# Grouped attention scores, with the main product on half of TensorE's rows, and a new order table

## The chip, the core and the metric

The kernel runs on one core of a Trainium2 chip. The metric is the device time of one launch in microseconds (us). TensorE (PE) does the matmuls, VectorE (DVE), ScalarE (ACT) and GpSimd (POOL) the elementwise work, and SyncE (SP) issues the DMA transfers. Each engine takes its own instructions in program order.

## What is computed

Pooled attention (query rows averaged in pairs) for 4 batches of 8 heads, 1152 keys, 576 pooled queries and head size 64. A feed-forward layer with a squared ReLU follows on 2304 tokens, 512 -> 2048 -> 512.

```python
q_pool = q.reshape(B, H, S // 2, 2, D).mean(axis=3)
scores = scale * np.matmul(q_pool, k.transpose(0, 1, 3, 2))
scores = scores - np.max(scores, axis=-1, keepdims=True)
attn = np.exp(scores)
attn = attn / (np.sum(attn, axis=-1, keepdims=True) + 1e-09)
x = np.matmul(attn, v)          # then heads side by side: (2304, 512)
h = x @ w_in
g = np.maximum(h, 0.0) ** 2
out = g @ w_out
```

## The kernel before, in words

The heads are handled in 16 pairs (pair n is two heads of one batch), and each pair in 9 chunks of 128 query rows, 144 chunks in all. Four chunks belong to the first head and four to the second; the ninth (`CH[j] is None`, here called the mixed chunk) holds the last 64 rows of each head. To keep float32 accuracy on float16 matmuls, numbers are split into a high and a low half (`hi`, `lo`). For keys, `k2` holds both halves beside each other, and a transposing DMA (KT) makes `kT`, in which each block of 128 keys has the 64 `hi` components on partitions 0 to 63 and the 64 `lo` components on 64 to 127. `qT` exists twice (index l): l = 0 as hi over lo, l = 1 with the halves swapped (made by the copies QX). So a full 128-row matmul with l = 0 gives hi x hi + lo x lo, and one with l = 1 gives lo x hi + hi x lo.

For one chunk the steps are: S (`scores`, L656 to L679, scores into one of two PSUM tiles `s0`, `s1` of three banks each), MX (L685, DVE, row maximum), MB (a small bias), EX (L709, ACT, exponential into P and row sums), HI and LO (L713 and L721, split of P), TR (L724, transposing DMA into PT). After four or five chunks a group PV (L869) multiplies PT by V; its two heads write to the two column halves of the array in turn. Pair 0 uses float32 scores (`scores4`, L653) in which two chunks, one of each head, lie on the two row halves of the array; pairs 1 to 15 use `scores`. In pairs 0 to 3 the transposition of P is done by TensorE (L750) and not by DMA. In `scores` a plain chunk has six matmuls of 512, 512, 128, 512, 512 and 128 columns. A mixed chunk has twelve, each with 64 stationary columns, and the two heads alternate matmul by matmul.

Since S alternates between `s0` and `s1`, S of chunk i waits for EX of chunk i - 2 (`back`).

The feed-forward work comes in 9 blocks of 256 tokens: normalisation (RV, RT L926, RB L948, XR L960, XQ L972, XN L980, XA, XD), eight H steps (L1033, 24 matmuls each) and eight O steps (L1082, 12 matmuls each). A block can start when all pairs that it needs are done, so it fills TensorE's time beside later chunks. XN needs XQ, XQ needs both XR, and those need both RB.

The order of all steps on all engines is a hand-over table, `ORDER`, three characters for each step (step, engine, buffer). `Plan.order` (L114) reads it; a step's `engs` says which engines it may run on, with planned durations that the kernel itself does not use.

Of the kernel before, what the change touches and what calls it, by code (L numbers as in the profile page):

```python
# [22 lines left out]
def cfg(k, d):  # L23
# [16 lines left out]
    "BU0O-8B7G1mWBF0BVGBH1BG8B80Bd0BIGBWEB9GBO1BeGBA0BP8BB8BQ1BJ0BR8Bm0BK8PrH1nOBfABnGPs0BX01oOPt8BY83S13TG"  # L40
    "Bg0BoDBv01pG3YSBh8BZ1BS0BwGBa8BT8Bb13cFBi0C201qGBj8Bc8Bx9Bk0C3G1r1Bl8CB01sGC48Bp01tJBr1CCGBq8Bs81u0CK0"
    "1vGCDEBy13dGB-01w8CT0BzG3KWB_GBt1CLGO_03eW1x83ZGCUGBu81yOCMACVB3P1P0GC503QG3aGC01Cc0C18C683V13UOC701z8"
    "Cl0C8G3kX3WGPu0PvGC911-83fWCAGPw0PxGCE13gWCFGCG0PyD3bW1_OCI1CHGCmGCJ8Pz03o9P11P-GCn8P_GQ0GQ1GCdGQ3E3XO"
    "208Q4GQ2GCN0CeDP2G3hOD10COG218CP13iGCR0Cu0CQG3jGCW1CS822OCvGCX83lWCf0Ch1Cg8Ci8CY0D2GCo1CZ8CwCCa0CbGD3G"
    "Cp8D80QvGD4A3nGQw0Cj1Qx8D9GD5R3qFCq0DF0Cr8Ck8D6ODAG3r0Cx1DBD3sGCyGCz03_8Cs1DM040G3xOCt8C-8DGGC_141WQ50"
    "D083mWDC8DHG3yGDIA3zGP312383-WDJKDKG248DDG47X42GQ68DNG25OQ78DT0DEW3p8DOGP4GQA0DPADUGQ88D7WDQD3u13tODa0"
    "Q9O3vGQBGQF14483wODVGDRG43ODW9DbGDSWQC8Q-0Dh0QG8Q_GDcOQD8DXOQH8Qy1DiGQK0DLWQI8QEODdAQzG45GR0FDo046GQL8"
    "DjGR11DeBQJG48WQP0R2GDYG4BDQM8DpGDZWDkCP51DfGQQ8Dq8QR8R3G4AGDgWQN8DlHQS8QU0DrADmGDs8QOGDnWQTGE00DtOP6G"
    "QV84DFDv0E1GQW84E1QZ04FGDuWR4GDwG4K84OOR6OE2G4PGQe1Dx8Qa84LGDyC49W4MGE3BDzQE704NWQb8EE0D-OE8GQj0EFGE98"
    "EA9D_WE4MEGOQc8EL0QXGEH8Qk0QYOEMG4WXEBCE5GEIDES04QWQf8ECGEN8Qg8P71EOAEJGE6WQh8EPRETGQiOEUGEQGEV9EZ0EKW"  # L50
    "QdOQl0P88EaG4C8ERWEW84SO4RGEg0EXO4H1EbGQm0EhGEcAEDWR5G4IGEi8EjEEdL4GOEn04a9EeOEu0EoGEYW4T8Qp1QnNEpG4JG"
    "4UGEqB4VGEfWEkAE_0EvGR78P90ElOF0GErC4XWR8GEw8Ex8Qq0F18EsGPA8QoWF2EEyDEtWFD0Qr04ZOFEGF3J4cFEmWEzGF4OF60"
    "FFG4d0Qs0F7GE-W4eGF8G4fG4nOF98R904jO4oGFGCF5WFHE4kGFR0RAGFIOFK0QtIRB8FSG4pWRJ04lG4YWFTGFLGFUDRE1FAC4mW"
    "FM8FBGRC8Ff0RDORF8FVBPB1FCWRG8FWGFN8RHOFgGRK8QuWRL84qO4rGFh8FY0FiD4vXRO0RIG4b8RMGFZGFj9RNOFJWFt0PCGFkO"
    "Fa8FbC4g14hGFm0FcAFXWFOLRT1RP8FnGFPORQ84s8FuGRR8Rd0Fo8FQWRSGFvOFpE4tGRU84uGRV8RY1FlWFdGFw8RWGFxJRXOG50"
    "RZ8FyG4wWFqCF-04iORe8PD14zDG6GFeWFrORf8Ra8F_GRb8Ri0Rg8PEG4yOG08RcGFzWG18RhO4_FRjG501GC051GG7OFsWRn0G89"
    "5AO52O5BGG2EGDGRk8G3OGJ04xWGE8Ro0GFAGKG56OG9BG4WGLGGG8GAGGQ0GMCPF1GRG5CWRl8GS8RmGGN957GGBWGOOGX0PG8Rp0"
    "4-85DGGHOGPWGYGGTE531GUCRq054G5EOGZGGIWRzHGaB58G5F8Gl055GRrNR-0Ge0GmG5IXRt05GGGfG59WGgGRu0GVGGhA5HGGn8"
    "R_8Gb95JWGs0Gi8GcGRv05MERsWGjOGtGGoDGWWRw0GpR5LGGuOGkW5OAGqO5P1Gz05QGPH15RGG-GGvC5VOGdWRxNGwDG_GGxGPI8"
    "GrWH08S20H40S3G5WGH1CS01S1G5Z8H2OT1GGyWS49H5GS515aGH68T20H78HB0S6G5bWS7G5XGH89HI0HCG5KWH9OPJ1S8GS9GHDG"  # L60
    "HJGHEBH3WHFLHK8SB85dG5cGHLASCGHP05YWT38HMOPK8HW0HQG5N8SD0HGOHXGHAWHRGHSCT41HNOSEGHY8T60HZBHd0T7GHHWT5G"
    "SF85S0SAOHk05TGT8ESGOHeG5e8T91SHOSI0HOWHlGHf8HgAHTPTAGTBG5UG5fGHr0SJ85hXHhMSK8SS1HsGHm8HaD5gGSL8Hn8HiG"
    "5iWSN0HbGRyWSMGHy0SO8HUGHcWSP8SX0SQ8HoI5kO5lBHtGHzGST8HjWHpGHuCPL1SRGSU8HvOSV8SYG5nFSWGHVWSZ8HwO5o0I30"
# [12 lines left out]
    "LG8UM8PZ06uWLHA74GL49LNG75GK_WUN8L5G7AOLI8LS0PaGLOCVC1VE0UOOLDW6x8VDGLZ0VFGLJO701LTGVGFUQ071GLU87FXLVE"
# [1294 lines left out]
```

## Time and profile before

| | us |
|---|---|
| median of 3 runs (775.4 to 783.15) | 780.74 |
| the profiled execution | 780.22 |
| its span | 778.1 |
| TensorE busy in the span | 736.7 |
| VectorE busy | 575.2 |
| ScalarE busy | 525.3 |
| GpSimd busy | 329.8 |

The profile is of one execution, whose own time is 2.1 us over its span. A view by stretches gives the busy time of each engine in each; the chain of work that ended last shows what the end depends on; a timeline lists the work of one engine in order of time, neighbours of one line merged, with the idle time ahead of each in brackets and what ended it. "PEclk" is the granted TensorE clock as a share of 2.4 GHz. In a timeline a matmul group's length includes the tail of its last matmul, about 0.16 us, which the next group overlaps; in the chain it does not.

### The profile page before, as it was taken

The numbers are of one execution on the slowest core, as the hardware profiler recorded it, in microseconds if no ns is written. First come the engines' busy times: TensorE is split into PE (matmuls) and PEld (weight loads), VectorE is DVE, ScalarE is ACT, GpSimd is POOL, SyncE is SP. The second block draws the span as 40 slices with busy tenths as digits, with TensorE's granted clock in tenths as the row PEclk, the third lists the DMA queues.
The fourth block names the chain that finished last, engine by engine and source line by source line (L and its number), as shares of the span: only waits on it lengthen the run. The fifth ranks groups of instructions, "written<-read, shape, count | busy, mean of one in ns | idle before, by whom it ended". The sixth has DMA issues, their size and how long they took to land. (4 is left out here: it accounts for less than half of the span.)

```text
span 778.1 us, 15243 instructions
## 1 busy us (share of the span) xinstructions
PE 736.7 (95%) x5998; PEld 485.7 (62%) x5998; DVE 575.2 (74%) x985; ACT 525.3 (68%) x821; POOL 329.8 (42%) x228
## 2 busy tenths in 40 slices
PE   6888899999899999899999999899999999999997
PEld 4555556557655775458666765586567658576763
DVE  4888999889788888789689888899788962404120
ACT  4988978989786887678877885779767732312140
POOL 1533412455365555464632644543476411204141
PEclk9999999999999999989999999999999999999999
DMA  8894782519999999999999999999999927000011
GB/s 282 279 244 136 219 227 89 122 44 194 208 207 206 198 208 201 213 206 183 214 221 214 199 210 192 203 211 208 225 190 188 195 47 131 1 1 14 15 42 40
DMA packets 324840, 128.96 MB, mean 166 GB/s; under 512 B 307104, under 2 KB 307872, under 8 KB 324768
## 3 DMA queue, kind: packets, MB, share of 16 engines
q1 hardware_dynamic: 324768, 127.98, 80.0%
q8 instruction: 47, 0.77, 0.4%
q14 instruction: 25, 0.20, 0.1%
HBM read 45.09 MB, written 4.72 MB: 64 GB/s over the span
## 5 line engine op out<-in xcount | busy, mean ns | idle before, releaser
L709 ACT ACTIVATE buf<-s,ca 128x1152 f32<-128x1152 f32 x144 | 175.2, 1217 | 57.1 <-DVE ca L695 18.6
L685 DVE TENSOR_SCALAR_CACHE_REDUCE s<-s,esc 128x1152 f32<-128x1152 f32 x135 | 190.5, 1421 | 29.1 <-PE s L674 25.7
L1033 PEld LDWEIGHTS <-w 128*128 128x128 f16 x1728 | 167.6, 98 | 26.7 <-issue 2.2
L721 POOL TENSOR_TENSOR buf<-buf,buf 128x1152 f16<-128x1152 f32 x49 | 121.8, 2489 | 100.8 <-ACT buf L713 78.6
L1082 PE MATMUL ba<-w,region 128*128 128x512 f16 x624 | 142.7, 379 | 0.0
L1082 PEld LDWEIGHTS <-region 128*128 128x128 f16 x864 | 82.4, 98 | 93.5 <-issue 1.7
L674 PE MATMUL s<-kT,qT 128*128 128x512 f16 x720 | 136.0, 329 | 1.8 <-ACT buf L709 1.7
L1033 PE MATMUL ba<-region,w 128*128 128x256 f16 x1128 | 129.4, 273 | 0.8 <-ACT region L1043 0.7
L674 PEld LDWEIGHTS <-qT 128*128 128x128 f16 x720 | 63.9, 100 | 58.8 <-issue 8.4
L869 PE MATMUL ba<-PT,v 128*64 128x320 f16 (+1 forms) x1296 | 85.0, 287 | 5.1 <-DMA PT<-buf 5.0
L721 DVE TENSOR_TENSOR buf<-buf,buf 128x1152 f16<-128x1152 f32 x59 | 81.2, 1385 | 9.7 <-ACT buf L713 9.1
L869 PEld LDWEIGHTS <-v 128*64 128x64 f16 x1296 | 70.7, 110 | 19.1 <-issue 9.2
L1060 POOL TENSOR_TENSOR region<-region 128x512 f16<-128x512 f32 x37 | 48.4, 1313 | 69.8 <-DVE region L1056 36.9
L713 ACT ACTIVATE buf<-buf 128x1152 f16<-128x1152 f32 x65 | 74.5, 1155 | 4.7 <-DVE buf L721 1.8
L1048 ACT ACTIVATE region<-region 128x512 f16<-128x512 f32 x72 | 44.2, 623 | 44.0 <-DVE region L1045 43.4
L750 PE MATMUL ba<-ident,buf 128*128 128x128 f32 x324 | 53.5, 289 | 12.6 <-ACT PT L760 5.7
L1082 PE MATMUL bt<-w,region 128*128 128x512 f16 x240 | 53.6, 379 | 0.0
L750 PEld LDWEIGHTS ba<-ident,buf 128*128 128x128 f32 x324 | 34.6, 143 | 29.2 <-ACT PT L760 12.2
L1056 POOL TENSOR_TENSOR region<-region 128x512 f32<-128x512 f32 x21 | 25.1, 1199 | 59.3 <-ACT region L1048 46.1
L1033 PE MATMUL bt<-region,w 128*128 128x256 f16 x408 | 46.0, 273 | 0.0
L760 ACT ACTIVATE PT<-ba 128x384 f32<-128x384 f32 x85 | 39.1, 489 | 9.9 <-PE ba L750 9.0
L282 POOL TENSOR_SCALAR buf<-buf,cols 128x1152 f16<-128x1152 f32 x19 | 26.6, 1400 | 36.8 <-ACT buf L709 19.4
(181 smaller groups left out, 915.6 us busy)
## 6 DMA issues: line engine op xcount, KB each, us to landing
raw<-in_q_dram SPq DMA_DIRECT2D x32, 288.0 KB, 3.8
raw<-in_k_dram SPq DMA_DIRECT2D x15, 576.0 KB, 4.7
region<-in_moe_w_in_dram SPq DMA_DIRECT2D x8, 1024.0 KB, 7.4
w<-in_moe_w_out_dram SPq DMA_DIRECT2D x8, 1024.0 KB, 6.0
raw<-in_v_dram SPq DMA_DIRECT2D x12, 576.0 KB, 4.6
out_dram<-buf SPq DMA_DIRECT2D x22, 128.0 KB, 2.4
v<-in_v_dram SPq DMA_DIRECT2D x4, 576.0 KB, 6.6
out_dram<-half SPq DMA_DIRECT2D x14, 128.0 KB, 2.5
```

What stands on the lines that cost most here:

```text
L674: nc.tensor.matmul(s[:, x, :w], lhsT=qt[:, l].rearrange("p c m -> p (c m)")[:, 128 * c0 + h : 128 * c0 + h + 255 : 2], rhs=rhs, **st)
L685: nc.vector.tensor_scalar(st3(), st3(), sc, 3e38, op0=ALU.mult, op1=ALU.min, accum_out=a[:, x : x + 1])
L709: nc.scalar.activation(P(), st3(), AF.Exp, bias=a[:, 1:2], scale=s1, accum_out=col)
L713: nc.scalar.activation(hl()[:, 0], P(), AF.Copy)
L721: e.tensor_tensor(out=hl()[:, 1], in0=P(), in1=hl()[:, 0], op=ALU.subtract)
L750: nc.tensor.matmul(t[:, y], lhsT=P()[:, c * 128 : (c + 1) * 128], rhs=ident, is_transpose=True, start=(y == 0), stop=(y == 2), skip_group_ ...
L760: nc.scalar.activation(out, t, AF.Copy)
L869: nc.tensor.matmul(px[h * 64 : (h + 1) * 64, 64 * r * (1 - h) : 64 * r * (1 - h) + N], lhsT=vv[:, h, kc, vl, :], rhs=p2(vi, r, h, 9 * pl + ...
L1033: nc.tensor.matmul(ph[:, f2], lhsT=w16[0][:, SLOT[f // 4], wl, a, f % 4 * 128 : (f % 4 + 1) * 128], rhs=xhl()[:, xl, a], start=(i == 0), s ...
L1048: nc.scalar.activation(gt[u][:, 0], rt[u % 2], AF.Square)
L1060: e.tensor_tensor(out=gt[u][:, 1], in0=rt[u % 2], in1=gt[u][:, 0], op=ALU.subtract)
L1082: nc.tensor.matmul(p[:, :DM], lhsT=g[:, gl, f % 2, tt * 128 : (tt + 1) * 128], rhs=w16[1][:, SLOT[f // 4], wl, f % 4], start=(f == 0 and g ...
```

## The change

Six edits. (1) For pairs 4 to 15 (`flip_`) the key blocks are laid out so that even blocks have hi over lo and odd blocks lo over hi (`kz`, used by `ka` and `kd`; the score columns and PV's V blocks are permuted to match, `PERM`). (2) In those pairs two chunks, one of each head, are scored together (`flipped`): first six full 128-row matmuls for the cross terms of both chunks (L730), then six 64-row matmuls for hi x hi, on the row half where that block's hi lies (L739); lo x lo is left out for these chunks. The order of chunks is `ORDF`, the mixed chunk seventh. S of such a group waits for EX of both chunks of the group before. (3) The mixed chunk still has twelve 64-column matmuls, all four products, but in loops with the head outside the column blocks (L722). (4) QX may run on any of three engines in all pairs. (5) Loads from pair 4 on and stores may be issued from ScalarE's queue (`AQ`). (6) A new `ORDER`.

```diff
 ORDER = (
-    "26W27W28W29X2C000W2E12DG2BG2G02F82I12H82K02MW2JG2L881006W02801O03882G2P18AG13W8382QG8408B904G86187G098"
+    "26W27W28W29X00W06W2C02E12DG2BO2G02FG2I12H82MW2K013W2J82L82NX03O01881002804G09882G05O8AG8382P107O0EW840"
...
-    ENG = ("PE", "ACT", "DVE", "POOL", "SP")
+    ENG = ("PE", "ACT", "DVE", "POOL", "SP", "AQ")
...
+    def queue(o):
+        return nc.scalar if o["eng"] == "AQ" else nc.sync
...
+        def kz():
+            return buf("k2", n).rearrange("p (a z d) -> p a z d", a=9, z=4), raw("k", n).rearrange("p (a z d) -> p a z d", a=9, z=2)
+
         def ka(o):
+            if n in flip_:
+                t, r = kz()
+                scaled(o, t[:, :, 0:4:3], r, tl["psc", n][:, 1, 0:1])
+                return
             scaled(o, k2()[:, :, :, 0, :], rk(), tl["psc", n][:, 1, 0:1])
...
-                add(("QX", n, z), {"SP": 850} if n in cfg("QXD", ()) else alt("QX", DVE=470, POOL=1500), [("QT", n)] + old, lambda o, z=z: qx(o, z), need)
+                add(("QX", n, z), {"DVE": 470, "POOL": 1290, "SP": 850}, [("QT", n)] + old, lambda o, z=z: qx(o, z), need)
...
+        def flipped(o):
...
+            full, half = slice(0, 128), (slice(0, 64), slice(64, 128))
+            if CH[j] is None:
+                for l in range(2):
+                    for h in range(2):
+                        for x, par, y, w in ((0, 0, 0, 4), (1, 1, 0, 4), (2, h, 1, 1)):
+                            nc.tensor.matmul(
+                                to(i, x, w)[half[h]], lhsT=qt[:, l, 8, h : h + 127 : 2], rhs=part(n, h, par, y),
+                                start=(l == 0), stop=(l == 1), skip_group_check=True,
+                            )
+                return
+            two = [(y, *CH[chunks[y][1]]) for y in both(i)]
+            for y, h, c0 in two:
+                for x, par, z, w in ((0, 0, 0, 4), (2, h, 1, 1), (1, 1, 0, 4))[:: 1 - 2 * h]:
+                    nc.tensor.matmul(
+                        to(y, x, w), lhsT=qcol(1 - par, full, h, c0), rhs=part(n, h, par, z),
+                        start=True, stop=False, skip_group_check=True,
+                    )
+            (a, ha, ca), (b_, hb, cb) = two
+            for y, h, c0, x, par, z, w in (
+                (a, ha, ca, 0, 0, 0, 4), (a, ha, ca, 1, 1, 0, 4), (a, ha, ca, 2, ha, 1, 1),
+                (b_, hb, cb, 1 - ha, 1 - ha, 0, 4), (b_, hb, cb, ha, ha, 0, 4), (b_, hb, cb, 2, hb, 1, 1),
+            ):
+                nc.tensor.matmul(
+                    to(y, x, w), lhsT=qcol(par, half[par], h, c0), rhs=part(n, h, par, z)[half[par]],
+                    start=False, stop=True, skip_group_check=True,
+                )
...
+        elif n in flip_:
+            if both(i)[0] == i:
+                back = [("EX", y - 2) for y in both(i)]
+                add(("S", i), {"PE": 1665 if len(both(i)) == 2 else 1115}, [("KT", n), ("QX", n, 0), ("QX", n, 1)] + back, flipped, i)
...
+    ORDF = [0, 7, 1, 8, 2, 5, 4, 3, 6]
...
+    flip_ = set(cfg("FLIP", range(4, 16)))
```

On TensorE, the scores of a plain chunk of pair 4 stood before as follows (`s0` and `s1` are the two score tiles; LDWEIGHTS loads the stationary operand of the matmul under it; the last number is the matmul's columns):

```order
L674 LDWEIGHTS qT0_105
L674 MATMUL s0_112<-kT0_103,qT0_105 128x512
L674 LDWEIGHTS qT0_105
L674 MATMUL s0_112<-kT0_103,qT0_105 128x512
L674 LDWEIGHTS qT0_105
L674 MATMUL s0_112<-kT0_103,qT0_105 128x128
```

and the second half of a group of two chunks of the same pair stands now:

```order
L730 MATMUL s1_113<-kT0_103,qT0_105 128x512
L739 LDWEIGHTS qT0_105
L739 MATMUL s0_112<-kT0_103,qT0_105 128x512
L739 LDWEIGHTS qT0_105
L739 MATMUL s0_112<-kT0_103,qT0_105 128x512
L739 LDWEIGHTS qT0_105
L739 MATMUL s0_112<-kT0_103,qT0_105 128x128
L739 LDWEIGHTS qT0_105
L739 MATMUL s1_113<-kT0_103,qT0_105 128x512
L739 LDWEIGHTS qT0_105
L739 MATMUL s1_113<-kT0_103,qT0_105 128x512
```

Both score tiles are now written in one go, and six matmuls of half the rows (L739; by the diff on the upper, lower, upper, lower, upper and lower rows in turn) stand where six full ones stood.

The mixed chunk of pair 4 on TensorE before (by the code, first and second of each equal two are the first and the second head, on the two column halves):

```order
L669 MATMUL s0_112<-kT0_103,qT0_105 64x512
L669 LDWEIGHTS qT0_105
L669 MATMUL s0_112<-kT0_103,qT0_105 64x512
L669 LDWEIGHTS qT0_105
L669 MATMUL s0_112<-kT0_103,qT0_105 64x512
L669 LDWEIGHTS qT0_105
L669 MATMUL s0_112<-kT0_103,qT0_105 64x512
L669 LDWEIGHTS qT0_105
L669 MATMUL s0_112<-kT0_103,qT0_105 64x128
L669 LDWEIGHTS qT0_105
L669 MATMUL s0_112<-kT0_103,qT0_105 64x128
```

and now:

```order
L722 MATMUL s0_112<-kT0_103,qT0_105 64x512
L722 LDWEIGHTS qT0_105
L722 MATMUL s0_112<-kT0_103,qT0_105 64x512
L722 LDWEIGHTS qT0_105
L722 MATMUL s0_112<-kT0_103,qT0_105 64x128
L722 LDWEIGHTS qT0_105
L722 MATMUL s0_112<-kT0_103,qT0_105 64x512
L722 LDWEIGHTS qT0_105
L722 MATMUL s0_112<-kT0_103,qT0_105 64x512
L722 LDWEIGHTS qT0_105
L722 MATMUL s0_112<-kT0_103,qT0_105 64x128
```

The 512, 512, 128 of the first head now stand together, and those of the second head behind them.

At one normalisation in the middle of the program, TensorE's order before had XN (L980) right behind the second RB (L948):

```order
L948 LDWEIGHTS pick_83
L948 MATMUL ba1_115<-ru_3205,pick_83 64x128
L980 LDWEIGHTS ones_80
L980 MATMUL ba1_115<-buf1_94,ones_80 128x256
L980 LDWEIGHTS ones_80
L980 MATMUL ba1_115<-buf1_94,ones_80 128x256
L980 LDWEIGHTS ones_80
L980 MATMUL ba1_115<-buf1_94,ones_80 128x256
L980 LDWEIGHTS ones_80
L980 MATMUL ba1_115<-buf1_94,ones_80 128x256
L926 LDWEIGHTS r2_3365
L926 MATMUL ba0_114<-negid_82,r2_3365 32x128
```

and now, with RB's rows (L1016) ahead of them, a score group and an RT (L994) stand between RB and XN (L1048):

```order
L739 LDWEIGHTS qT0_105
L739 MATMUL s1_113<-kT0_103,qT0_105 128x128
L994 LDWEIGHTS r2_3379
L994 MATMUL ba0_114<-negid_82,r2_3379 32x128
L1048 LDWEIGHTS ones_80
L1048 MATMUL ba1_115<-buf3_96,ones_80 128x256
```

XN has moved behind the scores of two chunks, and RT from behind XN to ahead of it.

## Rows read from the trace of the kernel before

**Rows 1.** The page: the span, and TensorE's busy time, share and matmuls.
```profile
span 778.1 us, 15243 instructions
PE 736.7 (95%) x5998; PEld 485.7 (62%) x5998; DVE 575.2 (74%) x985; ACT 525.3 (68%) x821; POOL 329.8 (42%) x228
```
**Rows 2.** Busy time by stretches of 40 us; its first line names the columns.
```profile
core 0: us, PE busy (x) PEld busy (x) DVE busy (x) ACT busy (x) POOL busy (x), PEclk, DMA share, GB/s
320.00:360.00 40.00, 34.83 (x326) 24.02 (x324) 34.30 (x64) 28.41 (x47) 18.73 (x14) 0.91 1.05 198
```
**Rows 3.** The chain that ended last: start us, length us, engine, tile, line, instructions.
```profile
543.18 0.97 PE s L669 x12
544.15 1.08 PE s L674 x6
...
583.96 1.10 PE s L669 x12
585.05 2.73 PE ba L1033 x24
587.78 0.97 PE s L674 x6
588.75 2.62 PE ba L1033 x24
```
**Rows 4.** TensorE's timeline, first 60 us: start, length, line, shapes, instructions.
```profile
27.53 2.10 PE L653 MATMUL s<-kT,qT 128*128 128x512 f32 x6
...
43.08 2.21 PE L653 MATMUL s<-kT,qT 64*128 64x512 f32 x12
```
**Rows 5.** What TensorE waited for from 200 us on: us, times, longest.
```profile
PE ba L980 <- ACT buf L972: 4.5, 1, 4.5
PE ba L869 <- DMA PT<-buf: 2.4, 2, 2.1
...
PE s L674 <- ACT buf L709: 0.5, 2, 0.3
```
**Rows 6.** TensorE's timeline from 318 to 362 us.
```profile
331.56 1.01 PE L980 MATMUL ba<-buf,ones 128*128 128x256 bf16 x4 [4.52 <-ACT buf L972]
...
332.73 4.02 PE L674 MATMUL s<-kT,qT 128*128 128x512 f16 x12
...
340.68 2.12 PE L674 MATMUL s<-kT,qT 128*128 128x512 f16 x12
...
349.23 0.61 PE L980 MATMUL ba<-buf,ones 128*128 128x256 bf16 x4
```
**Rows 7.** TensorE's timeline from 485 to 545 us.
```profile
498.31 3.85 PE L869 MATMUL ba<-PT,v 128*64 128x320 f16 x53 [2.12 <-DMA PT<-buf]
...
539.32 3.86 PE L869 MATMUL ba<-PT,v 128*64 128x320 f16 x54
```
**Rows 8.** ACT's timeline from 318 to 336 us.
```profile
327.39 1.22 ACT L709 ACTIVATE buf<-s,ca 128x1152 f32<-128x1152 f32 x1 [1.60 <-DVE region L960]
328.51 0.19 ACT L709 ACTIVATION_READ_ACCUMULATOR buf<-s,ca 128x1 f32 x1
...
331.42 0.28 ACT L692 ACTIVATE ca<-ca,cols 128x1 f32<-128x1 f32 x1
```
**Rows 9.** DVE's timeline from 318 to 336 us.
```profile
329.37 1.42 DVE L685 TENSOR_SCALAR_CACHE_REDUCE s<-s,esc 128x1152 f32<-128x1152 f32 x1
330.70 0.14 DVE L685 DVE_READ_ACCUMULATOR s<-s,esc 128x1 f32 x1
```
**Rows 10.** SyncE's timeline from 180 to 660 us.
```profile
180.50 15.05 SPq L724 DMA_TRANSPOSE PT<-buf  x4
...
591.20 30.88 SPq L724 DMA_TRANSPOSE PT<-buf  x10
626.59 1.86 SPq L1106 DMA_DIRECT2D out_dram<-buf  x2
638.66 14.48 SPq L724 DMA_TRANSPOSE PT<-buf  x5
```

More of the change, by code (lines that the diff above doesn't have):

```diff
@@ L357, in prep, with aq @@
         oldv = oldvs[0]
+        def aq(cost):
+            return {"AQ": cost} if n >= NP else {}
         def rk():
@@ L366, in rq, with load_kv @@
             return raw("q", n).rearrange("p (c r d) -> p c r d", c=9, r=2)
-        def load_kv(t, src):
-            nc.sync.dma_start(
+        def load_kv(o, t, src):
+            queue(o).dma_start(
                 out=t.rearrange("p h c d -> p h (c d)"),
@@ L376, in load_q @@
             for h in range(2):
-                nc.sync.dma_start(out=raw("q", n)[h : h + 127 : 2], in_=sv[h])
+                queue(o).dma_start(out=raw("q", n)[h : h + 127 : 2], in_=sv[h])
         prev = [] if not n else [("LQ", n - 1)] if n - 1 in full_v else [("LV", n - 1)]
@@ L678, in scores, with part, qcol, to @@
                             )
+        def part(n, h, par, y):
+            a = [x for x in range(9 * h, 9 * h + 9) if x % 2 == par]
+            a = a[4 * y : 4 * y + 4]
+            return kT(n)[:, a[0] : a[-1] + 1 : 2] if a else None
+        def flipped(o):
+            kt, qt = kT(n), qT(n)
+            def qcol(l, rows, h, c0):
+                return qt[rows, l].rearrange("p c m -> p (c m)")[:, 128 * c0 + h : 128 * c0 + h + 255 : 2]
+            def to(y, x, w):
+                t = sts[y % 2][:, x, : 128 * w]
+                return t.rearrange("p (a b) -> p a b", a=w)
+            full, half = slice(0, 128), (slice(0, 64), slice(64, 128))
[7 more added lines that the diff above has]
+                            )
+                return
+            two = [(y, *CH[chunks[y][1]]) for y in both(i)]
[14 more added lines that the diff above has]
+                )
         def smax(o):
@@ L1105, in st @@
                     ob = out[b_ * T : (b_ + 1) * T].rearrange("(p c) e -> c p e", c=9)
[L1106 removed]
+                    queue(o).dma_start(out=ob[c], in_=t[z * 64 : (z + 1) * 64])
             add(("OD", j, tt), {"DVE": 720}, [("O", j, tt, 3), ("XO", j)], od, at + 12 + 4 * tt, take=(("o", j, tt), ("buf", "half"), cfg("RO", 1)), give=("O", j, tt, 0))
[L1109 removed]
+            add(("ST", j, tt), {"SP": 1300, "AQ": 1400}, [("OD", j, tt)], st, at + 12 + 4 * tt, give=("o", j, tt))
     ring2 = {}
@@ L1281 @@
     lastr = {}
-    for n, pair, js in first + [(p, p, ORD) for p in range(NP, B * NP)]:
+    for n, pair, js in first + [(p, p, ORDF if p in flip_ else ORD) for p in range(NP, B * NP)]:
         p = preps[n]
```

157 lines of the change are left out of this document (81 added, 76 removed).

## Prediction

> **What bounds the kernel now.** I read the busy times first, then the chain that ended last, then TensorE's waits. TensorE is busy for 736.7 us of a span of 778.1 [rows 1], and in the chain its matmuls follow one another without a gap [rows 3]. From 200 us on it waits for little: 4.5 us once for ACT, 2.4 for transposing DMAs, 0.5 for exponentials of earlier chunks [rows 5]. The idle rest of the 41.4 us lies before 200 us and behind the last matmul. So the reader should see a kernel whose length, behind its first quarter, is the sum of its matmuls, and a change is worth what it does to that sum, unless it opens a wait. SyncE is nearly as full: it issues transposes without a pause from 180 us on, and its first long rest stands between 628.5 and 638.7 us [rows 10]. That is slack of 10 us near the end, so SyncE does not set the end yet.
>
> **The scores of plain chunks.** Six matmuls of a chunk take 0.97 us [rows 3]. Pairs 4 to 15 have 12 x 8 = 96 plain chunks: 93.1 us go. In their place come 48 groups. Their six full matmuls have the columns of one chunk: 0.97 x 48 = 46.6 us. Their six half-row matmuls have those columns again, and what they cost depends on whether the two row halves work side by side. The nearest row is the float32 scores of pair 0: one mixed chunk on all rows takes 2.10 us, and two chunks with the same number of columns each, one on either row half, take 2.21 together [rows 4]. Halves do run side by side there. In the new order upper and lower rows alternate, and each half gets 512 + 128 + 512 columns, half of the total; so I take 0.97 / 2 = 0.485 us, 23.3 us in all. The bounds are this and 0.97 us (nothing side by side, 46.6 in all).
>
> **Changes of mode.** A group of six takes 1.08 us when matmuls on column halves stand ahead of it and 0.97 otherwise, and an H step 2.73 and not 2.62 [rows 3]: each change of how the array is divided costs 0.11 us. Along TensorE's order the division (whole, column halves, row halves, small tiles) changes 126 times before and 211 times now, since each new group enters row halves and leaves them again. 85 x 0.11 = 9.4 us. The Trainium skill, TensorEngine Tiling (Array Packing), section Key Properties, speaks against such a change: changing the tiling mode, not just the tile, drains the engine. It gives no price; the trace agrees that there is one, and by its 0.11 us the sum stays as it stands here.
>
> **The mixed chunk.** Before, the heads alternate, two column halves work side by side, and 2304 columns of path take 0.97 us, or 1.10 with a change of mode ahead [rows 3]. Now three matmuls of one head stand together. Does TensorE start a matmul ahead of one that waits? At 331.56 us XN had waited 4.52 us for ACT, and the scores behind it began only at 332.73 [rows 6], although the exponential that they needed had ended at 328.70 [rows 8]. So starts keep to the program's order. Then the first head's 512 and 512 must have been taken before its 128 and the second head's first 512 can run beside each other; only the ends overlap. The path by columns is 1024 + 1024 + 1024 + 1024 + 128 = 4224 and not 2304, which at the same speed is 1.78 us, 0.81 more; twelve chunks: 9.7 us. The bounds are 0 (they overlap as before) and twice 0.97, 11.6 us. I take 9.7, since a queue that holds scores back for 4 us behind a waiting XN will not look ahead here either. The Trainium skill, TensorE: Matmul & The Clock Gate, section on packing small matmuls, says the same: matmuls start and end strictly first in, first out, and only weight loads are pulled ahead. The 4.52 us wait agrees.
>
> Sum on TensorE: 93.1 - 46.6 - 23.3 - 9.4 - 9.7 = 4.1 us less.
>
> **A wait that goes.** The one wait of 4.52 us has a price behind it: the granted clock of that stretch is 0.91 [rows 2], and the next two chunks took 4.02 us where two such chunks take 2.12, and XN 1.01 against 0.61 [rows 6]; that is 2.3 us at the lower of the two levels (1.2 GHz). In the new order a score group (0.97 + 0.485 + 0.22 = 1.7 us) and RT stand between RB and XN, as the last pair of listings shows. If XQ on ACT is as late as before, 2.8 us of wait remain. A wait of 2.12 us elsewhere did not lower the clock: 53 matmuls behind it took 3.85 us, and 54 take 3.86 without one [rows 7]. So I count 1.7 + 2.3 = 4.0 us won; the bounds are 0 (another wait of that length) and 6.8.
>
> **A wait that comes.** A group writes both score tiles, so it needs EX of both chunks ahead. From the end of a group: MX 1.42 + 0.14 us on DVE, twice, then the bias 0.28 and EX 1.22 + 0.19 on ACT [rows 8, 9], 4.8 us; beside a mixed chunk, where one chunk decides, 3.3. I laid the matmuls that stand between successive score groups of pairs 4 to 15 at the durations of their rows against this. Nine of 59 places have too little, together 2.7 us; in some ten more the margin is under 0.6 us, and DVE or ACT will often be in another instruction. Behind the waiting group stand H, O and PV, so TensorE loses all of it. I take 4 us, bounds 0 and 15 (a quarter of a microsecond at every place).
>
> **What costs nothing.** No transfer stands on ScalarE's queue in the new order, so edit 5 does nothing. The copies QX on SyncE grow by five, and transposes that follow a copy become two fewer of some thirty; this is covered by the 10 us rest at the end of SyncE's work [rows 10], and without it would be about 3 us late at the last PV. The key split keeps its element counts. The first four pairs are computed as before in another order; DVE's work there is the same, so I count 0, though ACT has slightly less.
>
> **Sum.** The profiled execution took 780.22 us, 2.1 over its span and 0.5 under the median of 780.74. 780.2 - 4.1 - 4.0 + 4.0 = 776.1 us, against the median 776.6. I predict 776 us.
>
> **Rivals.**
> (a) *The row halves do not run side by side with float16.* For it: no row shows it at float16, where columns pass twice as fast (0.97 us [rows 3] for what takes 2.10 in float32 [rows 4]). Against it: those rows themselves. It costs up to 23.3 us, 776 + 23 = 799; from a fifth of that (4.7 us) on the kernel is no faster than before. This is the slower case. 8%.
> (b) *The mixed chunk overlaps after all.* 9.7 us come back: 766. Against it is the held-back score group. 12%.
> (c) *Score groups wait throughout.* For it: both tiles are taken at once, and SyncE stays full, so a late transpose delays a buffer, then EX, then the next group. The place is each L730; at 0.25 us each, 15 us instead of 4: 787. Against it: ACT is busy for 68% and DVE for 74% [rows 1]. 20%.
> (d) *My sum, with waits between 1 and 8 us:* 773 to 780. 60%.
>
> **How the numbers follow.** A measurement here can tell about 1% from no change, 773 and 788.5 being the marks. Faster is (b), and about a quarter of (d), where the first 200 us gain from ACT's lighter load: 0.12 + 0.16 = 0.28. Slower is (a) and a quarter of (c): 0.13. Within 1%: 0.59. The range leaves out (a) and the outer ends of (b) and (c): 765 to 788; that of the likeliest case alone is 773 to 780.
>
> **What the new profile should show.** L730's and L739's twelve matmuls together 1.56 us in the chain, 1.67 with a change ahead; L739's starts in pairs. L722 at 1.8 to 1.9 us, not 1.1. TensorE's busy time near 733 us. XN's wait under 3 us and a granted clock of 1.00 there. TensorE's waits at L730 for EX (L773 of the new kernel) of 3 to 6 us. What would make me wrong: L739 near 1 us a group, L722 near 1.1, or waits at L730 above 10 us.

## The result

The changed kernel takes 787.67 us (median of 4 runs, 785.8 to 791.4) against 780.73 before (4 runs, 775.4 to 783.15): a ratio of 1.0112, 95% interval 1.0076 to 1.0147. It is slower by about 1%, where 776 us and no change were forecast. The profiled execution is the slowest of the four, 791.4 us with a span of 789.6, against 780.2 and 778.1; the traces are 11.5 us apart where the medians are 7 apart, so the rows below tell places better than sizes.

The page of the changed kernel, the span and TensorE's busy time:

```profile
span 789.6 us, 15253 instructions
PE 729.5 (92%) x5998; PEld 475.2 (60%) x5998; DVE 583.9 (74%) x988; ACT 521.5 (66%) x819; POOL 325.2 (41%) x222
```

TensorE works 7.2 us less than in [rows 1], and its idle time grew from 41.4 to 60.1 us. The busy time by stretches (the first line names the columns), of the changed kernel:

```profile
core 0: us, PE busy (x) PEld busy (x) DVE busy (x) ACT busy (x) POOL busy (x), PEclk, DMA share, GB/s
0.00:200.00 200.00, 170.53 (x1350) 109.60 (x1351) 167.51 (x291) 159.45 (x239) 78.84 (x56) 0.97 0.64 175
200.00:640.00 440.00, 414.60 (x3600) 270.86 (x3598) 368.09 (x613) 326.71 (x525) 218.73 (x139) 0.98 1.07 202
640.00:820.00 180.00, 144.34 (x1053) 94.75 (x1050) 48.26 (x86) 35.32 (x56) 27.61 (x28) 0.99 0.15 32
```

and of the kernel before:

```profile
0.00:200.00 200.00, 173.34 (x1386) 114.42 (x1388) 169.33 (x287) 165.37 (x253) 75.89 (x54) 0.99 0.67 184
200.00:640.00 440.00, 429.84 (x3634) 281.64 (x3631) 369.87 (x637) 330.60 (x521) 223.21 (x145) 0.99 1.06 197
```

In the 440 us in which chunks of pairs 4 to 15 run, TensorE was idle for 10.2 us before and is for 25.4 now. This is where the saving went. What it waits for there (us in all, times, longest), in the changed kernel:

```profile
PE ba L937 <- DMA PT<-buf: 5.7, 6, 2.1
PE s L730 <- ACT buf L773: 4.3, 5, 1.6
PE ba L510 <- DVE region L1113: 3.8, 2, 2.4
PE ba L510 <- DVE ru L1001: 3.1, 1, 3.1
PE ba L937 <- DVE ru L1001: 2.7, 1, 2.7
```

Against [rows 5] the wait of XN (4.5 us) is gone, but P x V (L937) waits more for transposed P, the score groups (L730) for exponentials, and several matmuls for DVE. The new steps themselves are as cheap as hoped. In the chain that ended last, the full and the half-row matmuls of a group (start, length):

```profile
639.24 1.08 PE s L730 x6
640.32 0.60 PE s L739 x6
```

and on TensorE's timeline a mixed chunk:

```profile
353.62 1.18 PE L722 MATMUL s<-kT,qT 128*64 128x512 f16 x12
```

The half rows run side by side: 0.60 us is 0.49 and the 0.11 of a change of mode. The mixed chunk takes 1.11 us from its first matmul to the next step's start at 354.73, no more than before [rows 3]; the 0.8 us that the prediction charged for it do not exist.

### The profile page after: what moved, and what is told of

Its sections match the earlier page's. It is cut to its first block, busy times and chain, and to the rows that moved or that the text cites. A ratio compares the mean times of both kernels' runs of the same rounds, so it can differ in the third digit from the quotient of the medians.

```text
span 789.6 us, 15253 instructions
## 1 busy us (share of the span) xinstructions
PE 729.5 (92%) x5998; PEld 475.2 (60%) x5998; DVE 583.9 (74%) x988; ACT 521.5 (66%) x819; POOL 325.2 (41%) x222
## 5 line engine op out<-in xcount | busy, mean ns | idle before, releaser
L785 POOL TENSOR_TENSOR buf<-buf,buf 128x1152 f16<-128x1152 f32 x63 | 153.9, 2449 | 151.5 <-ACT buf L777 87.9
L773 ACT ACTIVATE buf<-s,ca 128x1152 f32<-128x1152 f32 x144 | 175.3, 1218 | 40.9 <-POOL ca L759 10.8
L1150 PE MATMUL ba<-w,region 128*128 128x512 f16 x576 | 131.1, 379 | 0.7 <-DVE psc L520 0.7
L937 PE MATMUL ba<-PT,v 128*64 128x320 f16 (+1 forms) x1296 | 89.2, 296 | 9.5 <-DMA PT<-buf 5.7
L937 PEld LDWEIGHTS <-v 128*64 128x64 f16 x1296 | 76.2, 114 | 23.5 <-issue 13.5
L777 ACT ACTIVATE buf<-buf 128x1152 f16<-128x1152 f32 x58 | 67.0, 1156 | 8.3 <-DMA PT<-buf 4.6
L785 DVE TENSOR_TENSOR buf<-buf,buf 128x1152 f16<-128x1152 f32 x45 | 64.3, 1433 | 8.9 <-POOL buf L284 8.4
L1150 PE MATMUL bt<-w,region 128*128 128x512 f16 x288 | 64.0, 379 | 0.0
L730 PE MATMUL s<-kT,qT 128*128 128x512 f16 (+1 forms) x288 | 56.6, 330 | 4.8 <-ACT buf L773 4.3
L1128 DVE TENSOR_TENSOR region<-region 128x512 f16<-128x512 f32 x44 | 34.8, 800 | 11.1 <-POOL region L1124 9.3
L730 PEld LDWEIGHTS <-qT 128*128 128x128 f16 x288 | 25.4, 100 | 29.1 <-issue 9.6
L756 ACT ACTIVATE ca<-ca,cols 128x1 f32<-128x1 f32 x55 | 15.9, 289 | 35.5 <-DVE s L749 35.1
```

What stands on the lines that cost most here:

```text
L730: nc.tensor.matmul(to(y, x, w), lhsT=qcol(1 - par, full, h, c0), rhs=part(n, h, par, z), start=True, stop=False, skip_group_check=True,)
L773: nc.scalar.activation(P(), st3(), AF.Exp, bias=a[:, 1:2], scale=s1, accum_out=col)
L777: nc.scalar.activation(hl()[:, 0], P(), AF.Copy)
L785: e.tensor_tensor(out=hl()[:, 1], in0=P(), in1=hl()[:, 0], op=ALU.subtract)
L937: nc.tensor.matmul(px[h * 64 : (h + 1) * 64, 64 * r * (1 - h) : 64 * r * (1 - h) + N], lhsT=vv[:, h, PERM[h][kc] if n in flip_ else kc, vl ...
L1128: e.tensor_tensor(out=gt[u][:, 1], in0=rt[u % 2], in1=gt[u][:, 0], op=ALU.subtract)
```

## The experiments

Two readings stood against each other at first. T: SyncE's stream of transposes, full from the first one on, sets the pace of pairs 4 to 15, and TensorE's saving turns into idle time. P: the waits of the new groups and the new order on TensorE cost it, and SyncE does not matter. Every run is compared with the kernel before on the same chip; ratios below are against it, the changed kernel's is 1.0112, and where runs on different chips are set side by side, the difference of their ratios is taken (0.01 is 7.8 us).

**1. Does TensorE's work decide?** The second six matmuls of a group on all rows, which adds lo x lo again, as in the kernel before:

```diff
-  to(y, x, w), lhsT=qcol(par, half[par], h, c0), rhs=part(n, h, par, z)[half[par]],
+  to(y, x, w), lhsT=qcol(par, full, h, c0), rhs=part(n, h, par, z),
```

> The changed kernel and its order table, but the second six matmuls of a group of two chunks run on all 128 rows (so lo x lo is computed again, and six more columns' worth of TensorE time is spent). Each group takes 0.97 us and not 0.485 + 0.22 for its second half: 48 x 0.265 = 12.7 us more TensorE work. Theory T (from the first transposing DMA on, the chunks are paced by SyncE's full stream of transposes, and TensorE's saving has become idle time): 786 to 793 us, TensorE's idle time between 200 and 640 us falls from 25 to about 15 us. Rival P (TensorE's sum sets the time, and the loss comes from score groups that wait for both exponentials): 798 to 802 us.

793.57 us, 1.0181 (1.0145 to 1.0217). TensorE's busy time is 742.1 us, 12.6 more, and the ratio rose by 0.0069, 5.4 us: by the medians, less than half of what TensorE does more shows at the end (the intervals of the two ratios just touch, so the size is rough). Its idle time in the 440 us is 17.9 us and not 25.4. P's 798 and more is wrong, and T's upper end is just passed.

**2. Do the transposes decide?** Each transposes only the upper part (hi) of P, and P x V reads hi where it read lo; the lower part is left out. Once in the changed kernel, once in the one before:

```diff
-  nc.sync.dma_start_transpose(out=pslot(vi, j, False), in_=hl().rearrange("p l k -> p (l k)"))
+  nc.sync.dma_start_transpose(out=pslot(vi, j, False)[:, :9], in_=hl()[:, 0])
-  rhs=p2(vi, r, h, 9 * pl + kc, False),
+  rhs=p2(vi, r, h, kc, False),
```

> The changed kernel, with the transposing DMAs of P moving only the hi half, and PV reading the hi half where it read lo (so the product with P's lo half is replaced; same matmuls, half the transposed bytes). Theory T: with SyncE's stream relieved, TensorE's idle time between 200 and 640 us goes from 25 to 10 us or less: 765 to 775 us, and below the same edit of the kernel before. Rival P: the groups still wait for exponentials: 783 to 789 us.

> The kernel before with the same edit (transposes move P's hi half alone, PV reads hi where it read lo). Theory T: TensorE was full in the chunk phase already, so 772 to 781 us, slower than the changed kernel with this edit by 5 to 12 us. Rival P: 776 to 781 us, faster than the changed kernel with this edit.

765.02 us, 0.9812 (0.9761 to 0.9863), and 771.84 us, 0.991 (0.9879 to 0.9941). The changed kernel gains 0.030, 23 us, the old one 0.009, 7 us. The order of the two kernels turns round: with light transposes the change is worth 6.8 us. The same stretch of 440 us, first of the changed kernel with half transposes:

```profile
200.00:640.00 440.00, 431.88 (x3783) 282.98 (x3781) 369.12 (x634) 332.44 (x533) 227.98 (x143) 0.99 0.70 138
```

then of the old one:

```profile
200.00:640.00 440.00, 430.84 (x3642) 283.58 (x3641) 373.95 (x633) 325.15 (x512) 219.58 (x145) 1.00 0.67 133
```

TensorE's idle time is 8.1 us and not 25.4 in the first, 9.2 against 10.2 in the second. So transposes are behind most of the new idle time. A transpose took 1.57 us on SyncE here and 3.17 in the changed kernel (means of 108). The DMA share, the mean busy share of the core's 16 DMA engines, falls as well, from 1.07 to 0.70: this run relieves SyncE's queue and the DMA engines behind it at once, and does not say which of the two counts.

**3. More transposes in the old kernel.** The first three are issued twice:

```diff
+  for _ in range(2 if len(twice) < 3 else 1):
       nc.sync.dma_start_transpose(out=pslot(vi, j, False), in_=hl().rearrange("p l k -> p (l k)"))
+  twice.append(i)
```

> The kernel before, with each of the first three transposing DMAs of P issued twice (the same bytes to the same place): SyncE's stream is about 9 us longer at its very start, as the first transpose of the changed kernel is 9 us later. Theory T: 786 to 791 us, the delay is carried to the end. Rival P: 779 to 783 us, since TensorE's work is the same and 10 us of rest near the end of SyncE's stream take it up.

795.05 us, 1.0196 (1.0154 to 1.0238): 16 us for some 10 us of extra work, more than either reading said. TensorE's largest wait in it, from 180 to 300 us:

```profile
PE ba L873 <- DMA PT<-buf: 12.0, 2, 9.1
```

The first P x V of the stream stands still until its transposes land, and all behind it on TensorE with it. A late transpose can cost its whole lateness; that does not yet say that the changed kernel's are late in this way.

**4. Is it the start of the stream?** In the changed kernel's trace the first transpose of P starts 9.3 us later than before [rows 10]:

```profile
189.76 13.29 SPq L788 DMA_TRANSPOSE PT<-buf  x4
```

By the code the first group needs both score tiles, but the table is new as well; which of the two makes it late was not tried apart. Half transposes for pair 4 alone, pairs 4 to 9, and pairs 10 to 15 (lo of these pairs left out, as in 2); the diff is that of the first, the others have `4 <= n <= 9` and `n >= 10`:

```diff
-  nc.sync.dma_start_transpose(out=pslot(vi, j, False), in_=hl().rearrange("p l k -> p (l k)"))
+  hi = slice(0, 9 if n == 4 else 18)
+  nc.sync.dma_start_transpose(out=pslot(vi, j, False)[:, hi], in_=hl().rearrange("p l k -> p (l k)")[:, : 128 * hi.stop])
```

> The changed kernel, but the nine transposes of P of pair 4, the first nine of SyncE's stream, move the upper part (hi) alone, and pair 4's P x V reads hi where it read lo (left out: the lower part of pair 4's P). Everything later is untouched. A theory: the chunk phase is paced by SyncE's stream, and the changed kernel is late because its stream starts 9 us later. A whole transpose takes about 3.2 us and a half one about 1.6 (the kernel with all halves), so the stream catches up 9 x 1.6 = 14 us: 773 to 780 us, the last exponential of the chunk phase 9 to 14 us earlier than in the changed kernel. Rival P (what is lost comes from waits in the new order, spread over all pairs): work saved in one pair at the front returns as idle time, 785 to 790.

> The changed kernel; the transposes of pairs 4 to 9 (54 of 108) move hi alone, and P x V of these pairs reads hi where it read lo (left out: the lower part of their P). Theory L (transposes bind in the last pairs only, where TensorE waits most for them): 783 to 788. Rival E (they bind everywhere alike; all 108 gave 22 us): 774 to 779.

> The same for pairs 10 to 15. Theory L: 765 to 772. Rival E: 774 to 779.

787.01 us, 1.0097 (1.006 to 1.0134); 780.31, 0.9984 (0.9956 to 1.0012); 775.93, 0.996 (0.9938 to 0.9983). Pair 4 gives nothing that can be told from the changed kernel, so T in its form of a late start is wrong: the queue had 14 us less to do and the end did not move. Half the pairs give 10 and 12 us, together nearly the 23 of all: the gain is spread over both halves of the phase, as E had it. And 54 half transposes take 86 us of work (54 x 1.6) off SyncE for these 10 to 12 us, so the end is not the sum of SyncE's work either. What counts is that a transpose lands by the time that P x V, or the next user of its buffer, wants it.

**5. The copies QX.** The new table gives SyncE eight copies QX in pairs 5 to 15 (the expectation counted seven), where before it had none; in pairs 1 to 4 it has five, where before it had eight. All thirteen on DVE:

```diff
-  if o["eng"] == "SP":
+  if False:
       nc.sync.dma_start(out=t[a : a + 64, 1], in_=t[b_ : b_ + 64, 0])
   else:
-      e = nc.vector if o["eng"] == "DVE" else nc.gpsimd
+      e = nc.gpsimd if o["eng"] == "POOL" else nc.vector
```

> The changed kernel, but the copies QX that its order gives to SyncE are made by DVE (0.63 us each); nothing else is moved. Seven of them stand inside the stream of transposes. Theory T (SyncE's stream paces): each copy takes 0.55 us of SyncE, and the transpose behind one takes some 1.5 us more than one behind a transpose, so 4 to 14 us go: 774 to 784. Rival P (SyncE does not pace): DVE has 4.4 us more, nothing gained, 786 to 792.

783.15 us, 1.0043 (1.0019 to 1.0067): 4.5 us less by the medians, 5.4 by the ratios, within T's range. Then nearly the mirror image, the eight of pairs 5 to 15 on SyncE in the old kernel:

```diff
-  if o["eng"] == "SP":
+  if o["eng"] == "SP" or (n, z) in ((5, 0), (6, 1), (10, 1), (13, 1), (13, 0), (14, 0), (15, 1), (15, 0)):
```

> The kernel before, with the eight copies QX that the changed kernel's order gives to SyncE in pairs 5 to 15 made by SyncE here too (before, DVE made four of them and POOL four). Theory Q (a copy in the stream of transposes costs its 0.55 us and a dearer transpose behind it, and this reaches the end): 4 to 6 us more, 784 to 788. Rival R (the copies hurt only in the new order, whose groups come late): 779 to 783.

787.89 us, 1.0108 (1.006 to 1.0155): the copies alone make the old kernel as slow as the changed one. TensorE's timeline of this run shows 5 us of it at one place (start, length, line, instructions, wait ahead):

```profile
400.61 0.65 PE L674 MATMUL s<-kT,qT 128*128 128x512 f16 x3
404.35 0.65 PE L674 MATMUL s<-kT,qT 128*128 128x512 f16 x3 [3.09 <-DMA qT<-qT]
404.84 4.45 PE L1033 MATMUL ba<-region,w 128*128 128x256 f16 x24
```

and SyncE's timeline why:

```profile
397.93 3.50 SPq L724 DMA_TRANSPOSE PT<-buf  x1
401.47 0.58 SPq L566 DMA_DIRECT2D qT<-qT  x1
402.10 15.89 SPq L724 DMA_TRANSPOSE PT<-buf  x4
```

The copy stands behind a transpose of 3.5 us, is issued at 401.47 and lands 2.7 us later; TensorE, in the middle of a chunk's scores, waits 3.09 us, and the H step behind it takes 4.45 us, part of it at the lower clock (0.96 granted in the 40 us from 400 on, where before it is 1.00). In the trace of before the same chunk does not wait, and the same H step takes 2.78 us:

```profile
399.99 1.14 PE L674 MATMUL s<-kT,qT 128*128 128x512 f16 x6
400.97 2.78 PE L1033 MATMUL ba<-region,w 128*128 128x256 f16 x24
```

On DVE such a copy takes 0.63 us (631 ns, the mean of the ten from 200 to 640 us in the changed kernel's trace). Apart from the first of the stream (5.98 us, and 6.04 before), the transposes behind the copies took 2.6 to 3.9 us, nothing above the usual; the dearer transpose that my expectation priced is not there.

In the changed kernel this mechanism is not seen: in its trace TensorE waits for none of the copies on SyncE. With the copies on DVE P x V waits 2.7 us for transposes instead of 5.7, but these two traces are 9.9 us apart where the medians are 4.5 apart, and how the copies cost time there was not isolated.

**6. Any transfer, or these?** Stores of output blocks 0 to 5 on POOL's queue, in the kernel of run 5 (copies on DVE) and in the old one:

```diff
-  queue(o).dma_start(out=ob[c], in_=t[z * 64 : (z + 1) * 64])
+  (nc.gpsimd if j < 6 else nc.sync).dma_start(out=ob[c], in_=t[z * 64 : (z + 1) * 64])
```

> The changed kernel with the copies QX of SyncE on DVE (as in after_qxdve, 783) and the stores of output blocks 0 to 5 issued by POOL's queue; nothing is left out. Sixteen stores leave SyncE's stream. Theory Q (an ordinary transfer in the stream costs its 0.6 us and a dearer transpose behind it, together 0.6 to 1 us by the eight copies): 10 to 16 us, less what TensorE can't take: 768 to 776. Rival S (POOL is in order, and its splits of P queue behind a store that waits for its block): 785 to 795.

> The kernel before with the same stores on POOL's queue; twenty stores leave the stream. Theory Q: 12 to 20 us less on SyncE, of which TensorE, idle for 10 us of the phase, can take little: 772 to 778. Rival S: 785 to 795.

791.41 us, 1.0135 (1.0098 to 1.0172), and 778.2 us, 0.9996 (0.9972 to 1.002). Twenty of the stores that moved stood in the old kernel's 440 us; without them on SyncE it gains nothing on balance. That fits a stream in which a transfer has a price when somebody waits for it: scores wait for a copy QX, and in the trace of before nobody waits for a store. But POOL is busy for 346.0 us in this run and for 329.8 before, and a gain that this took back is not excluded. In the changed kernel POOL's queue made it worse; TensorE's largest wait there:

```profile
PE s L730 <- ACT buf L773: 10.1, 6, 4.8
```

The groups wait more for exponentials. That POOL's own work is held up behind the stores fits this, but was not shown.

**7. Loads and stores on ScalarE's queue** (loads of pairs 5 to 15, all stores):

```diff
-  return nc.scalar if o["eng"] == "AQ" else nc.sync
+  return nc.scalar if o["name"][0] in ("LK", "LQ", "LV", "ST") and (o["name"][0] == "ST" or o["name"][1] >= 5) else nc.sync
```

> The changed kernel with the loads of pairs 5 to 15 and all stores issued from ScalarE's queue, at the same places of the order; SyncE's stream keeps the transposes, the copies QX and the first loads. If the chunks are paced by the time that SyncE needs to issue (2.4 us of loads a pair, 26 us, and 15 us of stores in the chunk phase): 770 to 779 us. If they are paced by the DMA engines that all transfers share: 785 to 792 us, since the same bytes move. TensorE's sum with waiting score groups (P) says 786 to 790 us.

> The kernel before with the same edit (loads of pairs 5 to 15 and all stores from ScalarE's queue). If SyncE's issuing paces the chunks: 770 to 780 us, not below the changed kernel with this edit. If the shared DMA engines pace them: 778 to 786 us.

798.99 us, 1.0251 (1.0188 to 1.0315), and 792.55, 1.0154 (1.01 to 1.0207), and the transposes got no shorter (means of 3.22 and 3.13 us, against 3.17 and 3.21). TensorE waits longest for exponentials in both, 6.9 us at the groups of the first and 5.6 at L674 of the second, which fits loads that wait on ACT's in-order queue ahead of exponentials. The new cost hides what the relief of SyncE may be worth, so the pair of runs is inconclusive. It takes issuing off SyncE but no bytes off the DMA engines, whose share stays at 1.05 and 1.03; that transposes got no shorter would fit the DMA engines as the limit, but is no proof of it.

**8. Chunks taken out of the stream.** The P of four chunks transposed on TensorE, hi and lo written from PSUM by ACT and DVE:

```diff
+  nc.tensor.matmul(t[:, y], lhsT=P()[:, c * 128 : (c + 1) * 128], rhs=ident, is_transpose=True, start=(y == 0), stop=(y == 2), skip_group_check=True)
+  nc.scalar.activation(pt[:, 3 * x : 3 * x + 3, :], tl["tp", i, x], AF.Copy)
+  nc.vector.tensor_tensor(out=pt[:, 9 + 3 * x : 12 + 3 * x, :], in0=tl.pop(("tp", i, x)), in1=pt[:, 3 * x : 3 * x + 3, :], op=ALU.subtract)
```

> The changed kernel with four of its 108 chunks (41, 64, 89 and 110) taken out of SyncE's stream: their P is transposed by TensorE into PSUM (nine 128 x 128 transposes of float32, 1.5 us a chunk by those of the first four pairs), hi is written by ACT and lo by DVE from there; the split on POOL, ACT or DVE falls away for them. Nothing is left out of the computation. Theory T: SyncE's stream is 4 x 3.2 = 13 us shorter and TensorE has 25 us of idle time in the phase against 10 in the kernel before, so its 6 to 8 us more of work fit into it: 775 to 783. Rival P (TensorE's order of work sets the end, with its waits): 6 to 8 us more, 793 to 798.

804.71 us, 1.0315 (1.0264 to 1.0366), worse than both. TensorE's first waits from 200 to 640 us (L753 is the mixed chunk, L761 the first six matmuls of a group, L804 is EX):

```profile
PE s L761 <- ACT buf L804: 6.8, 7, 2.8
PE s L753 <- ACT buf L804: 4.0, 5, 1.8
```

Scores wait 10.8 us for exponentials, against 4.8 in the changed kernel. The twelve new steps on ACT, each of which waits for TensorE, would do that; it was not tried apart. So relief for SyncE that puts work in the way of exponentials loses more than it gains.

**9. The order of the mixed chunk.** The heads alternating again:

```diff
-  for h in range(2):
-      for x, par, y, w in ((0, 0, 0, 4), (1, 1, 0, 4), (2, h, 1, 1)):
+  for x in range(3):
+      for h in range(2):
+          par, y, w = ((0, 0, 4), (1, 0, 4), (h, 1, 1))[x]
```

> The changed kernel with the two heads of the mixed chunk alternating again, matmul by matmul, as in the kernel before. If TensorE starts a matmul on one column half ahead of waiting ones on the other (as far as three ahead), the twelve matmuls take 1.10 us either way and the time stays, 784 to 791. If starts kept to the program's order, as the prediction had it, twelve chunks would give back 0.8 us each, 778.

788.46 us, 1.0128 (1.0076 to 1.0181), no difference. And P x V of the old kernel in runs of one head, 27 matmuls long in pairs 4 to 6, 9 in pairs 7 to 9, 3 in pairs 10 to 12:

```diff
-  for i, (vl, pl, kc) in enumerate(ps):
-      for h in range(2):
+  run = 27 if n < 7 else 9 if n < 10 else 3 if n < 13 else 1
+  for g in range(0, 27, run):
+      for h, i in [(h, i) for h in range(2) for i in range(g, g + run)]:
+          vl, pl, kc = ps[i]
```

> The kernel before with PV's matmuls in runs of one head before those of the other: runs of 27 in pairs 4 to 6, of 9 in pairs 7 to 9, of 3 in pairs 10 to 12, alternating as before in pairs 13 to 15. If TensorE starts matmuls of the free column half ahead of waiting ones as far as the group reaches, all groups stay at 3.0 to 3.9 us. If it starts strictly in the program's order, runs of 27 take 6 to 7.3 us, runs of 9 5.7 to 7, runs of 3 4.5 to 5.5. If it looks ahead by some few matmuls, the short runs stay at 3.0 to 3.9 us and the long ones do not.

797.82 us in one run. Two of its P x V with runs of 27, of 256 and of 320 columns:

```profile
195.26 5.68 PE L871 MATMUL ba<-PT,v 128*64 128x256 f16 x54
220.06 7.01 PE L871 MATMUL ba<-PT,v 128*64 128x320 f16 x54
```

From the start of such a P x V to that of the next step it is 5.61 and 6.94 us; runs of 9 took 3.98 and 4.89, runs of 3 took 3.08 and 3.80, and alternating heads take 3.07 and 3.79. So TensorE starts a matmul on the free column half ahead of waiting ones on the other: over runs of 3 nothing is lost, over runs of 9 and 27 it is.

**10. The new table.** The new code under the old table, each operation behind those that it needs; the group behind the exponential of the chunk ahead of it and a step of TensorE, or without that step. The first lines of the table of the first of the two:

```diff
- "26W27W28W29X00W06W2C02E12DG2BO2G02FG2I12H82MW2K013W2J82L82NX03O01881002804G09882G05O8AG8382P107O0EW840"
...
+ "26W27W28W29X2C000W2E12DG2BG2G02F82I12H82K02MW2JG2L881006W02801O03882G2P18AG13W8382QG8408B904G86187G098"
...
```

> The changed kernel with the old table of orders: every operation stands where the old table had it, on the engine and in the buffer that the old table gave it, except where an operation of the new code needs one that stands behind it; such an operation is put right behind that one. The group of two chunks stands at the place of the old first chunk's scores, but behind the exponential of the chunk ahead of the group and one step of H, O or PV on TensorE, or at the place of the old second chunk's scores if that comes first. The copies QX of pairs 4 to 15 are not on SyncE then. Theory N (the new table costs what the half rows gain: copies on SyncE and a different order): without it 6 of the 12.7 us of the half rows come through, as in the comparison with whole rows: 770 to 778 us. Rival G (a group needs both score tiles, so any order has the wait, and the new table was made to soften it): a table made for single chunks fares worse, 788 to 800, with waits at the groups' first matmul for EX above 10 us in all.

> The same, but the group stands as early as it may: right behind the exponential of the chunk ahead of it in the order, without a step of TensorE between. Theory N: 770 to 780, since TensorE waits up to 1.4 us for that exponential at some groups. Rival G: 792 to 810.

910.32 us, 1.166 (1.1631 to 1.1689), and 904.85, 1.1587 (1.1562 to 1.1612). In the first, TensorE's largest waits from 200 to 760 us and its busy time there:

```profile
PE s L722 <- ACT buf L773: 19.1, 8, 4.7
PE s L730 <- ACT buf L773: 11.3, 11, 1.8
```

```profile
200.00:760.00 560.00, 450.66 (x3610) 287.10 (x3605) 384.40 (x627) 325.98 (x514) 216.60 (x143) 0.92 0.80 156
```

Scores wait 30 us for exponentials, TensorE is idle for 109 of 560 us, and its clock falls to 0.92. N falls: the new table is not a burden that can simply be taken off; under one not made for groups the new scores lose far more. How much of some 125 us the crude rearrangement makes and how much the groups is open.

## Why the prediction was wrong, by its steps

**"A change is worth what it does to that sum, unless it opens a wait."** This is the step that failed, in its second half: the only new wait that was priced was that of the score groups (4 us), and transfers that come late were put at nothing, because SyncE rests for 10 us near the end of its work [rows 10]. TensorE was busy for 95% and no other engine above 74% [rows 1], but transposes stand back to back on SyncE from 180 us on [rows 10], and the DMA share in [rows 2] was 1.05. The chain that ended last, in which the matmuls were read as standing without a gap [rows 3], reaches back only to 490 us, and there it goes through a transpose that P x V waited for:

```profile
491.98 6.29 DMA PT<-buf
498.27 0.04 issue
498.31 3.85 PE ba L869 x53
```

With 7.2 us less work on TensorE, 15.2 us more idle time appeared in the stretch of the chunks, and run 2 shows what it hung on: with half transposes most of the idle time is gone, and the change pays 6.8 us. Slack at the end says nothing about whether a transfer is in time in the middle.

**"What costs nothing": the copies.** The second failed step, and the largest single piece that a run isolates. I counted them as work of SyncE (3 us at most, covered). By the two runs of 5 they cost 4.5 us in the changed kernel and 7.8 in the old one. In the old one not their 0.6 us of issue but their lateness costs, 5 us of it at one place: a copy for which scores wait had been put on a queue that is hardly ever empty. In the changed kernel the cost is measured, but its way is open.

**The mixed chunk.** 9.7 us were charged and nothing was lost (run 9), so by its own terms the sum on TensorE was some 13.8 us in its favour and not 4.1. The reading from the XN that held scores back [rows 6] was about an instruction that waits for another engine; a matmul that only waits for its column half does not hold back one for the other half, if that is near. So what stands ahead of the prediction, that each engine takes its instructions in program order, is too strict for TensorE. The Trainium skill, TensorE: Matmul & The Clock Gate, section on packing small matmuls, has matmuls start strictly first in, first out; the measurement (1.11 us for runs of three, the same as alternating) differs, and it decides. With the mixed chunk right, the forecast would have been 766, still further off: the wrong rule was hidden behind a second error of the other sign.

**The half rows and the changes of mode** came as worked out: 0.49 us and 0.11. Rival (a) falls. TensorE's busy time was forecast near 733 us; it is 729.5, and 725.4 with the copies on DVE: 7.2 and 11.3 less than before, and not the whole 13.8, with parts of both at the lower clock.

**The wait that goes.** XN no longer waits 4.5 us for ACT. But the gain did not come, since two waits for DVE took its place in the same stretch (start, length, line, instructions, wait ahead, in the changed kernel):

```profile
333.44 0.35 PE L510 MATMUL ba<-acc,cols 128*128 128x2 f32 x2 [3.05 <-DVE ru L1001]
335.18 2.10 PE L730 MATMUL s<-kT,qT 128*128 128x512 f16 x6
342.21 6.52 PE L937 MATMUL ba<-PT,v 128*64 128x320 f16 x54 [2.66 <-DVE ru L1001]
348.66 1.15 PE L730 MATMUL s<-kT,qT 128*128 128x512 f16 x6
```

Six full matmuls take 2.10 us behind the first wait and 1.15 later; P x V takes 6.52 instead of 3.86: the lower of the two levels (1.2 GHz) again, and more of it than before: the granted clock of the stretch from 320 to 360 us is 0.83, where it was 0.91 [rows 2].

These waits, too, hang on the full queue. Ahead of the first of them DVE stood still for a load of q that SyncE had issued behind transposes:

```profile
323.03 1.30 SPq L382 DMA_DIRECT2D raw<-in_q_dram  x2
327.88 2.31 DVE L405 TENSOR_TENSOR raw<-raw 128x576 f32<-128x576 f32 x1 [1.91 <-DMA raw<-in_q_dram]
```

With half transposes for pairs 4 to 9 (run 4) this load is issued 10 us earlier, at 312.73, while TensorE is 5 us earlier; DVE does not wait for it, and TensorE's two waits are 0.5 and 0.3 us. With half transposes for pairs 10 to 15 alone they are still 3.0 and 2.6.

**The wait that comes** was sized well: 4 us forecast at the groups, 4.3 measured. Not forecast were 5.7 us of P x V for transposes, 3.3 more than before, and 9.6 us in the three largest waits for DVE, where before DVE held TensorE for 0.5.

**Rival (c)** gave the time, 787. Of its mechanism the part with the late transposes is right (run 2); the score groups themselves wait little. Its 20% were too few beside 60% for a sum that let no other engine speak.

**What stays open.** Without the copies the changed kernel is at 1.0043, so some 3 us over before remain (0.0043 x 780), and the saving of some 14 us that its sum gives with the mixed chunk put right is missing too. That transposes keep it back is shown in sum (run 2), spread over all pairs (run 4); which buffer, which load or which P x V loses how much is not, nor whether SyncE's issuing or the DMA engines behind it set the pace. Neither one queue's work nor one engine's adds up to the time: taking 14 us off SyncE at the start, or 20 stores, moved nothing. No kernel that does the whole computation was faster than the one before beyond the measurement; 778.2 us in run 6 (0.9996) is the same.

## What to carry to other kernels

Before a saving on the busiest engine is counted, shorten the next fullest queue in an experiment of its own: if the kernel gets faster (here the old one did, by 7 us), that queue shares the bound, and the saving may turn into idle time. A small transfer that someone waits for does not belong on a queue that is always full: its price is the time in the queue, its landing and what the clock loses behind the wait, in the old kernel 5 us at one place for a copy of 0.58 us of issue. The late one need not be one of the transfers that fill the queue: here it was also a load behind them. And slack is read where the wait is, not at the end of a stream.

## What the runs showed of the hardware

Matmuls on two column halves overlap fully in runs of three of one half (P x V 3.08 us) and lose more the longer the runs: 3.98 us for 9, 5.61 for 27, against 3.07 alternating. Two row halves in float16 run side by side, the second six matmuls of a group in 0.49 us (0.60 with a change of mode) beside 0.97 for full ones. A transpose of half the columns takes half the time on its queue (1.57 against 3.17 us).
